# All five engines of a fused attention and token-mixer kernel pinned to one order of steps, and part of its TensorE work removed

## The chip, the cores and the metric

The kernel runs on one core of one Trainium2 chip. Time is device time in microseconds (us) of that core; every number called a time is the median of several executions, and every "span" is the length of the one profiled execution, from its first to its last instruction. Engines: PE is TensorE's matmul side, PEld its weight loads, DVE is VectorE, ACT is ScalarE, POOL is GpSimd, SP is SyncE, which here only issues transfers.

## The reference

For 8 batches (8 heads, 576 positions, head width 64) the reference adds two attentions, and sends the sum through a token mixer:

```python
q_d, k_d, v_d = (t.reshape(B, H, S//4, 4, D).mean(axis=3) for t in (q, k, v))
out_d     = softmax(q_d @ k_d.T / sqrt(D)) @ v_d            # coarse, 144 positions
out_up    = np.repeat(out_d, 4, axis=2)
out_local = softmax(where(|i-j| < 4, q @ k.T / sqrt(D), -1e9)) @ v   # band
x  = (out_up + out_local) as [B, 576, 512]
wq, wk = x @ w_q, x @ w_k                                   # 512 -> 64
out = relu((wq @ wk.T / sqrt(64)) @ x) @ w_out
```

The product `(wq @ wk.T) @ x` is computed as `wq @ (wk.T @ x)`, so the mixer has a 64 x 512 middle matrix, `M2`.

## The kernel before

All matmuls are in fp16. Each batch goes through a cast stage and three stages, whose steps are Python closures:

- **cast**: q, k, the remainder rows r, and v from fp32 to fp16, on GpSimd.
- **a**: transposes of q, k, r on TensorE (PSUM tiles `pq`, `pk`, `pr`), evacuations to `qT`, `kT`; fourfold sums on GpSimd (`qd`, `kd`); masked scores of the band (`psc`) and their exponential `E`; the coarse v (`pv`, giving `vd` and `vblk`).
- **b**: coarse scores (`pcs`), coarse output (`pca`, giving `od`), its transpose (`pod`), band output (`pav`, giving `x`), its transpose (`px`, giving `xT`).
- **c**: `pw` (x times w_q and w_k, giving `wT`), transposed parts (`pwk`, and `pwd` before, `pws` after, for the coarse part), `pm2` (`pm` in the traces), `pmx` and `pmr` (relu, giving `rmx`), and the output matmuls `po` and `pol`.

Two pools of PSUM tiles serve all of that: three tiles of two banks (`ps`) and two of one bank (`psm`). A step that needs a tile waits until the tile's earlier user has been evacuated.

Stages of three different batches are interleaved by a rule of proportions, and only TensorE keeps the order in which the program emits its instructions. What the other four engines do when is left to the compiler's scheduler:

```python
class _InOrder:                       # cut
    def __getattr__(self, name):
        f_ = getattr(self._engine, name)
        return lambda *a, **k: self._tc.keep_in_program_order(f_(*a, **k))

TEN_ = _InOrder(tc, nc.tensor)

def merge(stages):
    steps = []
    for i, s_ in enumerate(stages):
        tot, at = sum(c for c, _ in s_), 0.0
        for c, f_ in s_:
            steps.append(((at + c / 2) / tot, i, f_))
            at += c
    for _, _, f_ in sorted(steps, key=lambda e: e[:2]):
        f_()
# ...
for i in range(B + 2):
    if i + 1 < B: st[i + 1]["in"] = load(i + 1)
    m_ = []                           # stage_c(i-2), stage_b(i-1), stage_a(i), stage_cast(i+1)
    # ...
    merge(m_)
```

`pw` multiplies the coarse output at full length, each coarse column read four times:

```python
for i in range(2):
    for r in range(4):
        TEN_.matmul(p_[:, i, 0:288], wqk16[:, r, :],
                    _ap(odT, r * T + 72 * i, [[row(odT), 128], [1, 72], [0, 4]]), start=(r == 0), stop=False)
    for r in range(4):
        TEN_.matmul(p_[:, i, 0:288], wqk16[:, r, :], xT[:, r, 288*i:288*i + 288], start=False, stop=(r == 3))
```

Many matmuls use a part of the array, for example 64 rows, 16 rows or 16 columns, so that TensorE changes the tile shape (rows x columns of the array in use) often.

The softmax here doesn't subtract the row's maximum and nothing guards it: scores larger than these inputs give would overflow.

## Time and profile before

The time before is 227.07 us (226.61 to 227.63, three runs).

| | before |
|---|---|
| span | 225.2 us |
| TensorE busy | 180.7 us, 80% |
| period of one batch in mid-kernel (start of `po` to start of `po`) | 23.06 us |
| TensorE work per batch, waits left out (estimate) | about 21.3 us |
| TensorE waits per batch (estimate) | about 1.8 us |
| first `pw` of the kernel | 51.8 us |

These are lines of the profile's page of the kernel before: busy time of each engine with its share and number of instructions; the busy tenths of TensorE in 40 slices of the span; the clock granted to TensorE in the same slices; the mean busy share of the DMA engines; and the shares of the chain of work that ended last.

```profile
span 225.2 us, 6421 instructions
...
PE 180.7 (80%) x2752; PEld 112.2 (50%) x2752; DVE 104.3 (46%) x262; ACT 103.1 (46%) x137; POOL 115.9 (51%) x131
...
PE   0336077759988998899898989898989998999681
...
PEclk9999999857999999999999999999999999999999
...
PE 49%; DVE 17%; POOL 16%; ACT 10%; issue 3%; DMA 3%; POOLq 0%; DVEq 0%; ACTq 0%
```

The row of digits shows two kinds of time. From slice 10 on (about 51 us) TensorE is at 8 or 9 tenths nearly without interruption: there the period is TensorE's own work plus a few short waits. Before that it is idle more than half the time. The chain gives GpSimd 16%; all its pieces on GpSimd lie in the first 73 us. (The row PEclk shows 9 where the profile holds no record of the clock. In this run the first record is at 36.4 us.)

The next lines are the windows view of the kernel before over two periods: start and end, length, busy us of each engine (and instructions), granted clock, DMA share, GB/s.

```profile
88.30:111.30 23.00, 21.47 (x344) 13.31 (x344) 12.02 (x29) 12.64 (x18) 13.52 (x13) 1.00 0.81 214
111.30:134.40 23.10, 21.52 (x345) 13.36 (x345) 12.11 (x29) 12.71 (x18) 13.62 (x13) 1.00 0.80 208
```

TensorE is busy 21.5 us of 23, no other compute engine more than 13.6. And here is what TensorE waited for in the whole of that run (some groups left out; us in total, times, longest):

```profile
PE pv L27 <- POOL v_0_136 L163: 9.0, 3, 7.9
PE pq_230 L27 <- POOL q_142 L156: 8.6, 1, 8.6
PE pr L27 <- POOL r_144 L158: 4.1, 1, 4.1
PE pv L27 <- POOL v_1_138 L163: 3.7, 3, 2.6
PE psc L27 <- DVE rmx L445: 2.1, 6, 0.3
PE pw L27 <- DVE xT L368: 1.5, 7, 0.3
PE pv L27 <- POOL v_2_140 L163: 1.1, 2, 0.6
```

The long ones (7.9, 8.6, 4.1 and 2.6 us) are single waits of the start, for GpSimd's casts. The rest come once per batch: 0.6 us at `pv` for GpSimd's cast of v, up to 0.3 us at `psc` and at `pw`. So waits are small in mid-kernel, and to make it much shorter TensorE must have less to do.

### The profile page before, as it was taken

How to read it: one execution, taken by the hardware profiler on the slowest of the kernel's cores; microseconds unless marked ns; L12 is line 12 of the kernel's file. 1: busy time of each engine (PE TensorE's matmuls, PEld its weight loads, DVE VectorE, ACT ScalarE, POOL GpSimd, SP SyncE). 2: the span in 40 equal slices, each digit the busy share in tenths (PEclk: the TensorE clock that was granted, in tenths of full speed). 3: DMA queues.
4: the chain of work that ended last, by engine and by line, in shares of the span. 5: the costliest groups of instructions: out<-in, count | busy, mean ns of one | idle time of the engine just before them, and what ended most of it. 6: DMA issues, size and time to landing. Idle time of an engine off the chain costs nothing.

```text
span 225.2 us, 6421 instructions
## 1 busy us (share of the span) xinstructions
PE 180.7 (80%) x2752; PEld 112.2 (50%) x2752; DVE 104.3 (46%) x262; ACT 103.1 (46%) x137; POOL 115.9 (51%) x131
## 2 busy tenths in 40 slices
PE   0336077759988998899898989898989998999681
PEld 0223046536555664566455745574557455656330
DVE  6005046523466337354726472646364546477022
ACT  2154036413843593458444853475456554331331
POOL 3587991993079607970698059904990393000000
PEclk9999999857999999999999999999999999999999
DMA  6999989979974599659974997599731022104105
GB/s 184 288 198 328 317 165 263 266 150 243 249 173 146 156 349 163 194 146 341 170 207 129 332 175 167 189 309 206 195 136 27 3 92 82 41 3 157 53 0 210
DMA packets 74027, 40.54 MB, mean 180 GB/s; under 512 B 52432, under 2 KB 68880, under 8 KB 74000
## 3 DMA queue, kind: packets, MB, share of 16 engines
q1 hardware_dynamic: 73920, 40.12, 68.7%
q8 instruction: 21, 0.34, 0.7%
q14 instruction: 6, 0.05, 0.1%
q10 hardware_dynamic: 80, 0.03, 0.1%
HBM read 30.67 MB, written 9.44 MB: 178 GB/s over the span
## 4 chain that ended last, share of the span: by engine, by line
PE 49%; DVE 17%; POOL 16%; ACT 10%; issue 3%; DMA 3%; POOLq 0%; DVEq 0%; ACTq 0%
PE po L27 11%; PE pw L27 8%; ACT kT L184 5%; DVE xT L368 5%; DVE rmx L445 4%; PE pav L27 3%; PE pmx L27 3%; PE pod L27 3%; DMA q_72<-in_q_dram 3%; PE psc L27 3%; DVE os L470 3%; PE px L27 2%; PE pca L27 2%; POOL qd L207 2%; PE pwd L27 1%
## 5 line engine op out<-in xcount | busy, mean ns | idle before, releaser
L27 PE MATMUL po<-wo_98,rmx 128*128 128x512 f16 x128 | 30.4, 380 | 2.3 <-ACT rmx L443 0.6
L27 PEld LDWEIGHTS <-rmx 128*128 128x128 f16 (+1 forms) x160 | 14.1, 100 | 18.1 <-ACT rmx L443 0.7
L368 DVE COPY xT<-px 128x928 f16<-128x928 f16 (+1 forms) x32 | 14.3, 453 | 11.4 <-PE px L27 11.0
L348 DVE RECIPROCAL rz<-pav 128x8 f32<-128x8 f32 x40 | 8.1, 202 | 24.7 <-PE pav L27 23.9
L27 PEld LDWEIGHTS <-wqk_97 128*128 128x128 f16 x128 | 12.2, 100 | 6.5 <-DVE xT L368 2.9
L313 DVE RECIPROCAL rc<-pca 128x8 f32<-128x8 f32 (+1 forms) x16 | 3.2, 201 | 22.6 <-PE pca L27 22.6
L468 ACT COPY os<-po 128x1024 f32<-128x1024 f32 x8 | 8.1, 1012 | 11.8 <-PE po L27 10.6
L445 DVE TENSOR_SCALAR rmx<-pmx 128x1024 f16<-128x1024 f32 x8 | 9.8, 1224 | 7.3 <-PE pmx L27 7.3
L27 PE MATMUL pw<-odT,wqk_97 128*128 128x288 f16 x64 | 11.0, 297 | 1.5 <-DVE xT L368 1.5
L470 DVE COPY os<-po 128x1024 f32<-128x1024 f32 x8 | 9.7, 1216 | 4.8 <-ACT os L468 3.0
L443 ACT ACTIVATE rmx<-pmx 128x1024 f16<-128x1024 f32 x8 | 8.2, 1024 | 5.9 <-PE pmx L27 5.9
L27 PE MATMUL pw<-xT,wqk_97 128*128 128x288 f16 x64 | 10.8, 293 | 0.0
L27 PE MATMUL psc<-id_67,neg 64*128 64x232 f16 (+1 forms) x80 | 8.7, 280 | 2.1 <-DVE rmx L445 2.1
L329 DVE COPY odT<-pod 128x576 f16<-128x576 f16 x8 | 3.7, 458 | 14.4 <-PE pod L27 14.4
L27 PE MATMUL psc<-qT,kT 64*64 64x58 f16 (+1 forms) x640 | 10.3, 200 | 0.0
L482 ACT COPY ol<-pol 64x512 f32<-64x512 f32 x8 | 4.6, 579 | 11.6 <-PE pol L27 11.6
L27 PEld LDWEIGHTS <-kT 64*64 64x64 f16 x640 | 7.6, 114 | 4.4 <-issue 3.8
L27 PE MATMUL pq_230<-id_67,q_142 128*128 128x128 f16 x16 | 1.9, 312 | 8.6 <-POOL q_142 L156 8.6
L27 PE MATMUL pv<-v_0_136,P_149 128*32 128x512 f16 x3 | 1.3, 449 | 9.0 <-POOL v_0_136 L163 9.0
L27 PE MATMUL pol<-wo_98,rmx 128*64 128x512 f16 x32 | 8.4, 385 | 0.0
L242 ACT ACTIVATE E_0_122<-psc 128x928 f16<-128x928 f32 x4 | 3.8, 946 | 9.7 <-PE psc L27 9.7
L256 ACT CAST vd_0_195<-pv 128x512 f16<-128x512 f32 x4 | 2.4, 588 | 12.5 <-PE pv L27 12.5
(561 smaller groups left out, 518.3 us busy)
## 6 DMA issues: line engine op xcount, KB each, us to landing
out_dram<-os SPq DMA_DIRECT2D x16, 512.0 KB, 3.0
v_75<-in_v_dram SPq DMA_DIRECT2D x10, 128.0 KB, 4.2
v_215<-in_v_dram SPq DMA_DIRECT2D x10, 128.0 KB, 4.4
v_401<-in_v_dram SPq DMA_DIRECT2D x10, 128.0 KB, 3.7
v_779<-in_v_dram SPq DMA_DIRECT2D x10, 128.0 KB, 3.9
v_1258<-in_v_dram SPq DMA_DIRECT2D x10, 128.0 KB, 4.2
v_1737<-in_v_dram SPq DMA_DIRECT2D x10, 128.0 KB, 3.7
v_2216<-in_v_dram SPq DMA_DIRECT2D x10, 128.0 KB, 3.8
```

What stands on the lines that cost most here:

```text
L27: return lambda *a, **k: self._tc.keep_in_program_order(f_(*a, **k))
L184: nc.scalar.copy(t_[:, :, 0:512].rearrange("p j (t f) -> p j t f", f=4), g["p" + key].rearrange("p a (j f t) -> p (a j) t f", j=2, f=4))
L207: nc.gpsimd.tensor_tensor(qd, s_[:, :, :, 0], s_[:, :, :, 1], op=ALU.add)
L242: nc.scalar.activation(E.rearrange("p a n h w -> p a (n h) w")[:, :, :, 0:w], p_[:, :, 0:len(pr_) * W].rearrange("p a (x w) -> p a x w", w=w),
L329: nc.vector.tensor_copy(odT, p_[:, 0:4 * T].rearrange("p (r t) -> p r t", r=4))
L348: nc.vector.reciprocal(rz[:, n], _ap(p_, 64, [[row(p_), 128], [512, 2], [65, 4]]))
L368: nc.vector.tensor_copy(g["xT"][:, 2 * i:2 * i + 2, o:o + m * w].rearrange("p r (m w) -> p r m w", m=m), p_[:, :, lo:lo + 64 * m].rearrang ...
L443: nc.scalar.activation(d_, p_, ACTF.Relu)
L445: nc.vector.tensor_scalar_max(d_, p_, 0.0)
L468: nc.scalar.copy(os_, p_)
L470: nc.vector.tensor_copy(os_, p_)
L482: nc.scalar.copy(ol_, p_[0:64])
```

## The change

The intent is to fix the order of steps on all five engines. The order is one list of steps with batch lags, said to come from a search over a model of the program; evacuations of PSUM are divided between ScalarE and VectorE by a table. The diff is larger than that description: it also removes and pads work. This is its core, with cuts:

```diff
-    TEN_ = _InOrder(tc, nc.tensor)
+    pe = _InOrder(tc, nc.tensor)
+    sp = _InOrder(tc, nc.sync)
+    pool = _InOrder(tc, nc.gpsimd)
+    act = _InOrder(tc, nc.scalar)
+    dve = _InOrder(tc, nc.vector)
 # ... every instruction of a step goes through these; load() is split in load_qk and load_v
+    load_qk(1)                       # q and k of batch 1 are asked for before w_out
 # ... batch 0: casts of q, r on dve, of k on act; its k sums on dve; w_out's casts on act
+    EVAC = {"qT": "a", "kT": "a", "rem": "d", "vd0": "a", "odT": "a", "xT0": "d", "xT1": "d",
+            "wTd": "a", "wk": "d", "wd": "a", "M2": "a", "mx0": "a", "mx1": "d", "mxr": "a",
+            "og0": "a", "og1": "a", "ol": "d"}
 # ... before: odT, mxr, og1 on VectorE; wk, ol on ScalarE
-                    TEN_.matmul(p_[:, i, 0:288], wqk16[:, r, :],            # fourfold coarse half of pw
-                                     _ap(odT, r * T + 72 * i, [[row(odT), 128], [1, 72], [0, 4]]), ...)
+        def wtd():                                                          # once, on 144 columns
+            for r in range(4):
+                pe.matmul(p_[:, 0:T], wqk16[:, r, :], odT[:, r, :], start=(r == 0), stop=(r == 3))
+            evac("wTd", wd, p_[:, 0:T])
+            dve.tensor_tensor(wT[...], p_[:, :, 0:288] ..., wd broadcast 4x, op=ALU.add)
-                for od, lo, hi in ((g["od0"], 0, 128), (g["od1"], 128, T)):  # second one 16 rows
-                    TEN_.transpose(p_[:, r * T + lo:r * T + hi], od[:, 128*r:128*r + 128], id16[...])
+                for i in range(2):                                           # both 128 rows
+                    pe.transpose(p_[:, 256*r + 128*i:256*r + 128*i + 128], g["od"][i][...], id16)
 # ... the same kind of padding in pcs, pca, pws, pm2, pmx, pmr, pol
-    merge(m_)
+    ORDER = [
+        (-2, "og1"), (-1, "wtd"), (0, "sums"), (1, "cast_qk"), (-1, "wt"), (0, "vd"), (0, "mask0"),
+        (0, "score0"), (-1, "wks"), (2, "load_qk"), (1, "cast_v"), (0, "mask1"), (-1, "wkt"), (0, "score1"),
+        (0, "mask2"), (0, "av0"), (-1, "m2"), (0, "av3"), (0, "score2"), (0, "av1"), (-1, "mx0"), (0, "av2"),
+        (0, "cs0"), (-1, "mx1"), (0, "cs1"), (0, "av4"), (0, "weights"), (-1, "mxr"), (1, "tq"), (0, "ca0"),
+        (2, "load_v"), (-1, "og0"), (0, "ca1"), (1, "tk"), (1, "tr"), (-1, "ol"), (0, "xt0"), (0, "xt1"),
+        (0, "odt"),
+    ]
+    for i in range(-3, B + 3):
+        for lag, name in ORDER:
+            if 0 <= i + lag < B and (i + lag, name) not in done:
+                steps[i + lag][name]()
```

So three things come together: (1) less TensorE work, by the single coarse half and by fewer changes of tile shape; (2) another order; (3) pins on four more engines.

## The prediction

> **What bounds it now.** In mid-kernel a batch takes 23.06 us (the starts of the output matmuls `po`: 88.3, 111.3, 134.4, 157.4 us in the timeline). TensorE is the busiest engine there (18.5 to 19.0 of every 20 us, by windows; VectorE 10.4 to 10.9, ScalarE 9.8 to 11.6, GpSimd 10.5 to 13.6). From start-to-start times of matmuls at 60 to 160 us: 216 ns for 512 columns, 123 for 288, 56 for 128. Each change of tile shape adds about 95 ns (512 columns: 311 instead of 216; 128 columns: 150 instead of 56), about 44 changes per batch. [...] Summed, TensorE needs about 21.3 us per batch, and about 1.8 us are waits (px to pv 0.64, pav to psc 0.42, psc to po 0.32, pcs to pw 0.26). Outside the steady part: `pq` of the third batch starts only at 55.0 us (two batches started; GpSimd casts and sums, in the chain of waits, and DMA share 0.9 to 1.3), and after the last batch's `pw` at 207 us come 18 us.
>
> **What the change does.**
> 1. `pw` loses its fourfold coarse half: 8 matmuls of 288 go, 4 of 144 come: 0.98 - 0.25 = -0.73 us.
> 2. Padding of pod, pca, pcs, pm, pmx, pol to full shape, and the order, leave about 17 shape changes: roughly -2.5 us. My sum for the new order is 18.3 us of TensorE per batch.
> 3. VectorE takes the coarse add, wk and ol; ScalarE odT, wTd, mxr, og1: ScalarE 13.6, VectorE 12.3, GpSimd 13.8 us per batch. None binds. DMA packets took 18.2 us of 16 engines per batch, so DMA stays under, nearly filled.
> 4. All engines are strictly ordered. Walking the order by hand with these durations (0.26 us from last matmul to evacuation, 3 double-bank PSUM buffers), `av1` waits 0.9 us for the exp of `score2` (same buffer), cs0, mx1, av4 together 0.8, `tq` 0.5 for the relu of mx1: 2.2 us of waits. Period 20.5 us.
> 5. The last stage lags one iteration less. Start: `vd` stands first, so TensorE waits for v's cast, about 20 us for batch 0 and about 40 for batch 1 (its v lands about 38, as before). ScalarE waits for wo (now behind q, k of batch 1), around 29 us. TensorE is idle before 40 us and may run at the low clock there (before: 0.50 at 45 to 50 us).
>
> **Sum.** Second iteration ends at about 59 us; five iterations of 20.5 to 161.5; one without the next batch's transposes, 18.5, to 180; last stage, output and landing 18 to 19: 199; times run 2 us over the span: **200 us**, 8 in 10 between **190** and **211**. Chances: faster by over 2% 0.95, within 2% 0.04, slower 0.01.
>
> **What would show it.** Mid-kernel period 20 to 21 us; `pw` 8 per batch; TensorE gaps at pav and pq, ended by ScalarE's E and VectorE's rmx; TensorE above 60% of the chain; a TensorE gap before batch 1's `pv` ended by GpSimd's v cast; matmul busy sum lower than 180.7 us.
>
> **What would make it wrong.** DMA not keeping up once a batch takes 20 us (then the period is above 21 and gaps end on casts that waited for DMA); waits overlapping less than in my walk; or the start being better hidden (then down to 190).

## The result and the profile after

The changed kernel takes 193.46 us (193.05 to 194.9, four runs) against 227.05 us. The ratio is 0.852, with a 95% interval of 0.847 to 0.857. The outputs are correct.

The lines of the page after, in the order used above; the line "q8 instruction" is of the DMA queues (packets, MB, share of the 16 engines) and is needed later:

```profile
span 192.7 us, 6374 instructions
...
PE 155.5 (81%) x2720; PEld 104.0 (54%) x2720; DVE 114.8 (60%) x286; ACT 110.7 (57%) x140; POOL 107.7 (56%) x122
...
PE   0034448885899989998999899989998999898790
...
PEclk9999555999789999999999999999999999999997
...
q8 instruction: 21, 0.34, 0.7%
...
PE 68%; DVE 17%; ACT 7%; issue 4%; POOL 2%; ACTq 0%; DVEq 0%
```

TensorE's busy time fell by 25.2 us, its share of the chain rose from 49 to 68%, and GpSimd nearly left the chain (16 to 2%). Two periods in the windows view after:

```profile
93.30:112.60 19.30, 18.52 (x345) 12.44 (x342) 12.32 (x29) 13.22 (x18) 11.96 (x13) 1.00 0.95 239
112.60:131.90 19.30, 18.52 (x345) 12.43 (x342) 12.32 (x29) 13.23 (x18) 13.47 (x12) 1.00 0.92 241
```

A period is 19.30 us (before 23.06), and the DMA engines are now 92 to 95% busy in it (before 80%). They are not the limit yet: none of TensorE's waits between 88 and 157 us ends on a transfer or on a cast. TensorE's waits of the whole run (some groups left out):

```profile
PE pq_236 L27 <- DVE q_229 L27: 12.6, 1, 12.6
PE pv L27 <- POOL v_0_147 L27: 5.2, 1, 5.2
PE psc L27 <- DVE vblk_201 L27: 2.8, 1, 2.8
PE pav L27 <- issue: 2.3, 1, 2.3
PE pmx L27 <- ACT E_0_135 L27: 1.2, 3, 0.4
PE pmx L27 <- ACT E_1_145 L27: 1.2, 3, 0.4
```

Only one wait of size is left per batch, 0.4 us at the first `pmx`, which takes over the PSUM tile of the last band score and has to wait for its exponential E. Two more are 0.2 us each (`pcs` for an x, `pav` for Ec). With what the start-to-start times of the matmuls leave for waits, a period reads as follows; the work column is an estimate, summed from start-to-start times of the trace with the waits taken out.

| | period | TensorE work | waits | shape changes per batch in the trace |
|---|---|---|---|---|
| before | 23.06 | 21.3 | 1.8 | 40 |
| after | 19.30 | 18.2 | 1.05 | 18 |

One of the 18, from 112 to 128 rows in `pm`, costs only 10 ns (226 instead of 216 ns between starts), so 17 count.

Where the 32.5 us of span went, by the starts of `pw`: 12.0 us until the first `pw` (51.8 to 39.8), 19.1 us between the first and the last (155.4 to 136.3), 1.4 us after the last (18.0 to 16.6).

What a change of tile shape costs can be read from the timeline after. Columns are start in us, length of one in us, engine, source line, operation, output and inputs, tile shape, form, number; the bracket gives idle time before it and what ended it.

```profile
45.03 0.38 PE L27 MATMUL pm_847<-x_444,wk_206 128*128 128x512 f16 x1
45.25 0.38 PE L27 MATMUL pm_847<-x_543,wk_206 128*128 128x512 f16 x1
45.56 0.38 PE L27 MATMUL pav<-v_1_149,E_1_141 64*64 64x65 f16 x12
...
45.97 0.23 PE L27 MATMUL pav<-v_1_149,E_1_143 64*64 64x65 f16 x3
48.52 0.38 PE L27 MATMUL pav<-v_1_149,E_1_143 64*64 64x65 f16 x13 [2.33 <-issue]
```

The 512-column matmuls start 0.21 to 0.22 us apart, but the first 64 x 64 one starts 0.31 us after the last of them: about 95 ns more for the change from 128\*128 to 64\*64. The last two lines show another thing: a hole of 2.3 us between matmuls of one and the same tile, with nothing that the profile could name as waited for. It is taken up in the experiments on the start.

### The profile page after: what moved, and what is told of

Same layout as the page of the kernel before. It is cut to its first block, busy times and chain, and to the rows that moved or that the text cites. A ratio compares the mean times of both kernels' runs of the same rounds, so it can differ in the third digit from the quotient of the medians.

```text
span 192.7 us, 6374 instructions
## 1 busy us (share of the span) xinstructions
PE 155.5 (81%) x2720; PEld 104.0 (54%) x2720; DVE 114.8 (60%) x286; ACT 110.7 (57%) x140; POOL 107.7 (56%) x122
## 4 chain that ended last, share of the span: by engine, by line
PE 68%; DVE 17%; ACT 7%; issue 4%; POOL 2%; ACTq 0%; DVEq 0%
PE po L27 15%; PE psc L27 6%; PE pav L27 5%; PE pw L27 4%; PE px L27 4%; PE pca L27 4%; PE pol L27 4%; DVE kd_127 L27 3%; PE pv L27 2%; PE pcs L27 2%; ACT kT L27 2%; PE pod L27 2%; DVE rz L27 1%; PE pws L27 1%; PE pwd L27 1%
## 5 line engine op out<-in xcount | busy, mean ns | idle before, releaser
L27 ACT COPY os<-po 128x1024 f32<-128x1024 f32 x16 | 16.2, 1012 | 14.7 <-issue 8.3
L27 PE MATMUL po<-wo_91,rmx_227 128*128 128x512 f16 x64 | 15.3, 379 | 0.6 <-ACT rmx_227 L27 0.6
L27 PE MATMUL po<-wo_91,rmx_212 128*128 128x512 f16 x64 | 15.1, 379 | 0.0
L27 DVE COPY xT<-px 128x928 f16<-128x928 f16 (+1 forms) x32 | 13.8, 451 | 0.6
L27 PE MATMUL pq_236<-id_67,q_229 128*128 128x128 f16 x16 | 1.9, 312 | 12.6 <-DVE q_229 L27 12.6
L27 PEld LDWEIGHTS <-rmx_227 128*128 128x128 f16 x80 | 7.2, 98 | 8.1 <-ACT rmx_227 L27 0.7
L27 PE MATMUL psc<-qT,kT 64*64 64x58 f16 (+1 forms) x640 | 11.4, 198 | 0.0
L27 PEld LDWEIGHTS <-rmx_212 128*128 128x128 f16 x80 | 7.2, 98 | 6.6
L27 PEld LDWEIGHTS <-wqk_90 128*128 128x128 f16 x96 | 8.3, 98 | 3.7 <-issue 0.9
L27 ACT COPY odT<-pod 128x448 f16<-128x448 f16 (+1 forms) x16 | 5.6, 402 | 6.3 <-PE pod L27 6.3
L27 PE MATMUL pw<-xT,wqk_90 128*128 128x288 f16 x64 | 9.2, 286 | 0.0
L27 PEld LDWEIGHTS <-q_229 128*128 128x128 f16 x16 | 1.6, 146 | 12.6 <-DVE q_229 L27 12.6
L27 POOL CAST v_0_147<-v_79 128x2560 f16<-128x2560 f32 x1 | 3.1, 3129 | 9.3 <-DMA w_92<-in_moe_w_k_dram 9.3
L27 DVE TENSOR_TENSOR wT_219<-pw,wTd 128x576 f16<-128x576 f32 x4 | 3.0, 758 | 8.6 <-ACT wTd L27 8.6
L27 DVE COPY ol<-pol 64x512 f32<-64x512 f32 x8 | 5.5, 682 | 4.3 <-PE pol L27 4.3
L27 DVE TENSOR_TENSOR wT_204<-pw,wTd 128x576 f16<-128x576 f32 x4 | 3.0, 758 | 8.0 <-ACT wTd L27 6.6
L27 DVE TENSOR_SCALAR rmx_227<-pmx 128x1024 f16<-128x1024 f32 x4 | 4.9, 1224 | 4.1 <-PE pmx L27 4.1
L27 POOL CAST v_1_149<-v_255 128x2560 f16<-128x2560 f32 x1 | 2.3, 2323 | 8.6 <-DMA v_255<-in_v_dram 8.6
```

## The experiments

Three theories of the gain were open. The first: less TensorE work explains it (25 us less busy time). The second: the order explains it. The third: the pins explain it, above all one on some engine whose order the scheduler gets wrong. Experiments e1, e4, e9 and e10 take order and pins apart; e2 and e3 put work back in the new order; e5 undoes the division of evacuations; e6, e7, e8, e11 and e12 are on what is left. Each is an edit of the changed kernel, and all gave correct outputs. The kernel before took 227.69 us in the rounds of e1 to e4, 226.94 in those of e5 to e8, 227.48 in those of e9 to e12.

### e1: only TensorE pinned, all else as after

```diff
-    sp = _InOrder(tc, nc.sync)
-    pool = _InOrder(tc, nc.gpsimd)
-    act = _InOrder(tc, nc.scalar)
-    dve = _InOrder(tc, nc.vector)
+    sp, pool, act, dve = nc.sync, nc.gpsimd, nc.scalar, nc.vector
```

> The changed kernel, but only TensorE is pinned; the scheduler orders the other four engines again. In the built program it changes little: ScalarE puts wTd before the copy of og1, GpSimd casts v before q and k, VectorE's setup is shuffled. Theory A (the gain is less TensorE work plus a TensorE order that leaves few waits): 193.5 us, within 192 to 197. Theory B (pinning all five engines to one order is what pays): above 200 us, with new TensorE gaps in mid-kernel and a period above 20 us instead of 19.3.

Measured: 249.72 us, ratio 1.095 (1.090 to 1.100). The new order without the pins is slower than the kernel before, and 56 us slower than with them. This is in theory B's range. One group of TensorE's waits in this run stands out, and so does the row of the granted clock:

```profile
PE pv L27 <- POOL v L257: 41.4, 8, 7.2
...
PEclk9995569559995799659985899569975999579999
```

`pv` waits for the cast of v in every batch, up to 7.2 us. GpSimd's timeline of one period of e1 shows why:

```profile
120.57 2.11 POOL L295 TENSOR_TENSOR sum<-qT 128x1152 f32<-128x1152 f16 x1 [13.81 <-DVE qT L238]
...
127.70 2.32 POOL L257 CAST v<-v 128x2560 f16<-128x2560 f32 x1
...
147.98 2.11 POOL L295 TENSOR_TENSOR sum<-qT 128x1152 f32<-128x1152 f16 x1 [13.73 <-DVE qT L238]
```

and GpSimd's timeline of the changed kernel, one period:

```profile
112.49 2.32 POOL L27 CAST v_2_151<-v_1970 128x2560 f16<-128x2560 f32 x1 [3.79 <-DMA out_dram<-os]
116.57 2.11 POOL L27 TENSOR_TENSOR sum_2573<-qT 128x1152 f32<-128x1152 f16 x1 [1.76 <-DVE qT L27]
...
123.71 1.89 POOL L27 CAST q_2583<-q_2183 128x2048 f16<-128x2048 f32 x1
```

In the changed kernel the cast of v stands before the sums, early enough for `vd`, which the new order puts first. Left to the scheduler, GpSimd does the sums of q and k first, which need that batch's transposes, and only then the cast of v, which `pv` needs. TensorE, pinned, stops at `pv`; so the next batch's transposes come late; so GpSimd sits idle 13.8 us. A ring through two engines makes the period 27.4 us, though no engine is full. The low clock is part of it: from 73 us on it is 0.5 for 10.2 of each 27.3 us, and from the start of `pv` to that of `pr` (the last transposes before the sums) TensorE takes 17.0 us here and 13.6 in the changed kernel. So an estimated 3.4 us of the 8.1 us by which the period is longer come from the clock; in e9, where the wait is gone, the clock stays at 1.0 in mid-kernel.

### e9: TensorE and GpSimd pinned

```diff
-    sp = _InOrder(tc, nc.sync)
     pool = _InOrder(tc, nc.gpsimd)
-    act = _InOrder(tc, nc.scalar)
-    dve = _InOrder(tc, nc.vector)
+    sp, act, dve = nc.sync, nc.scalar, nc.vector
```

> TensorE and GpSimd pinned, ScalarE, VectorE and the DMA queue left to the scheduler. In the slow run with TensorE alone pinned, the scheduler had put GpSimd's cast of v behind the sums of the same batch, while TensorE's order has vd, which needs that cast, first in the iteration: tr(b), sums 7.1 us, cast 2.3 us, vd(b) became a loop of 27.4 us. Theory C (that one place on GpSimd is the whole loss): back to 193 to 197 us, period 19.3 to 19.5. Theory B (each pinned engine matters): above 200 us.

Measured: 196.3 us (195.95 to 197.06), ratio 0.864 (0.860 to 0.867), period 19.6 us. The time is in theory C's range, the period just above its 19.5. Pinning GpSimd gives back 53 of the 56 us that e1 lost. Pins on SyncE, ScalarE and VectorE together are worth the last 3 us: the period of e9 is 0.33 us longer than after from the second on, all of it between `pv` and the next `psc`, where its trace has a wait that it puts down to VectorE's wT (0.3 us per batch) and the trace after has none.

### e2: the coarse half back in `pw`

```diff
-        def wtd(): ...                # 4 matmuls of 144 columns, added on VectorE
+        for i in range(2):            # in pw: 8 matmuls of 288 columns on the fourfold odT
+            for r in range(4):
+                pe.matmul(p_[:, i, 0:288], wqk16[:, r, :], _ap(odT, ..., [[row(odT), 128], [1, 72], [0, 4]]), ...)
-            dve.tensor_tensor(wT..., p_..., wd..., op=ALU.add)
+            dve.tensor_copy(wT..., p_...)
```

> The coarse half goes back into the 288-column matmuls of pw (16 instead of 8 per batch), wtd goes, VectorE copies instead of adding; the order stays. Theory A (TensorE is still the bound in every batch, so its work counts in full): 8 x 123 - 4 x 62.5 = +0.73 us per batch, period 20.0 us, total 199 us (197.5 to 200.5). Theory B (the order makes the gain; this work is hidden by waits that exist anyway, about 1 us per batch): below 196 us.

Measured: 200.87 us (200.11 to 202.16), ratio 0.882 (0.878 to 0.887), period 20.3 us. That is just above theory A's range; theory B is out. The single coarse half is worth 7.4 us in the new order, 1.0 us per batch, more than the 0.73 us that the matmuls alone make. In the traces these are 0.98 - 0.25 = 0.73 us, as expected; the other 0.26 us lie between `pv` and the next `psc`, a wait for wT as in e9.

### e3: ten shape changes per batch put back

```diff
-                    pe.transpose(p_[...128 columns...], g["od"][1][:, 128*r:128*r + 128], id16)
+                pe.transpose(p_[...32 columns...], g["od"][1][96:128, 128*r:128*r + 128], id16[96:128, 96:128])
-                pe.matmul(p_, rmx[:, r * S + 512:r * S + 640], wo16[:, r, :], ...)       # pol, 128 wide
+                pe.matmul(p_[0:64], rmx[:, r * S + 512:r * S + 576], wo16[:, r, :], ...)  # 64 wide
```

> The changed kernel with two paddings undone: od1's transposes take 32 rows (8 more changes of tile shape per batch) and pol takes 64 columns (2 more). No matmul is added; four get fewer columns. Theory A (a change of tile shape costs about 95 ns of TensorE): +10 x 0.095 - 0.1 = about +0.8 us per batch, period 20.1 us, total 200 us (197 to 202). Theory B (shape changes are free, only columns and order count): 193 us or slightly less.

Measured: 200.47 us (199.52 to 200.97), ratio 0.879 (0.875 to 0.884), period 20.2 us, in theory A's range. Ten more shape changes per batch cost 7.0 us: 7.0 / 80 is 88 ns for each, beside the 95 ns of the trace. The padding that e3 undoes costs at most an estimated 0.22 us per batch (four transposes of 128 columns, which start 56 ns apart in the trace; 512 columns start 216 ns apart on 64 columns of the array as on 128), so it is nearly free here beside the 0.88 us per batch that leaving these matmuls small costs. In the new order, work taken from TensorE comes back as time almost one for one.

### e4: the new work in the old order, only TensorE pinned

The steps of the changed kernel are emitted by the old rule of proportions; `wtd` and `wt` share the old weight of `pw`, a mask and its score that of the old score.

```diff
-    sp = _InOrder(...); pool = ...; act = ...; dve = ...
+    sp, pool, act, dve = nc.sync, nc.gpsimd, nc.scalar, nc.vector
-    ORDER = [ ...the searched list... ]
+    ORDER = old_order()      # stage c at lag -2, b at -1, a at 0, casts at +1, merged by shares
```

> The changed kernel's steps, work, padding and evacuation split in the old order (the proportional merge of the stages, last stage two iterations behind), with only TensorE pinned, as before. 21 shape changes per batch in the built program instead of 17 (before: 39 in the trace). Theory A (most of the gain is TensorE work taken away): TensorE needs about 18.6 us per batch plus waits as before, 1.8 us: period 20.4 us, total 203 to 212. Theory B (the searched order is most of the gain): period above 21.5 us, total above 217.

Measured: 213.15 us (212.06 to 214.15), ratio 0.935 (0.929 to 0.941), period 22.1 us: the total lies between what the two theories expected, the period in theory B's range. Its TensorE waits between 88 and 157 us, where the trace after has 0.4 us per batch at `pmx` and little else:

```profile
PE pv L27 <- ACT E L337: 2.0, 3, 0.7
PE po L27 <- DVE x L450: 1.7, 3, 0.6
PE pmx L27 <- ACT M L230: 1.6, 3, 0.5
PE pwk L27 <- DVE wT L499: 1.4, 3, 0.5
PE pav L27 <- DVE rmx L234: 1.3, 3, 0.4
```

So a period of e4 is an estimated 18.6 us of work (three or four more shape changes than after) and 3.4 us of waits. The old order had 2.7 us of work per batch removed and paid only 1.0 us; 1.6 us turned into waits for evacuations (3.4 us per batch against 1.8). That TensorE, with less work in between, comes to each evacuation sooner is the reading of these waits, not measured. The list ORDER places some other batch's matmuls between a matmul and the one that needs its evacuation; that this is what removes the waits is read from the list and the two tables of waits, no run isolates it.

By the starts of `pw`, the 14.5 us by which the span of e4 (210.7 us) is shorter than before are 3.9 at the start (first `pw` at 47.9 us), 9.2 between the first `pw` and the last, and 1.4 at the end. Of the other 18 us to the changed kernel 8.1 are at the start and 9.9 between the first `pw` and the last. What moving batch 0's casts off GpSimd and asking for q and k of batch 1 early bring at the start was not measured apart: e4 has both.

### e10: the same, all five engines pinned

```diff
-    ORDER = [ ...the searched list... ]
+    ORDER = old_order()      # all five _InOrder kept; the weights' casts at the end of the list
```

> The old order of steps with the new work, now with all five engines pinned to it (w_out's cast at the end of the first iteration). With only TensorE pinned this took 213 us at a period of 22.1, about 3.4 us of it waits of TensorE for evacuations of the step just before. Theory A (the waits lie in the order of the steps themselves): 208 to 216 us. Theory B (pinning the other engines repairs them): below 205 us.

Measured: 224.0 us (222.95 to 225.15), ratio 0.985 (0.981 to 0.989), and nearly the same waits in mid-kernel as e4, with a period of 21.7 to 22.8 us. Neither expectation held. The loss against e4 is in the start: `pwd` of the first batch starts at 57.5 us, in e4 at 45.9. TensorE's waits in the first 60 us of e10 include these two:

```profile
PE pcs L27 <- POOL qd L27: 10.4, 1, 10.4
PE pcs L27 <- POOL kd L27: 6.5, 1, 6.5
```

Pinned GpSimd holds the sums of a batch behind casts of the next batch, whose data have not landed: its timeline has the sums of batch 0 starting at 30.0 us, behind casts that waited for q and k from memory until 22.7 and 27.6 us, and those of batch 1 at 49.7 us, behind a cast that waited for k until 47.3 us. Pins are not good in themselves: they keep a good order and a bad one alike. (The place of the weights' casts differs between e4 and e10 too; the two waits above do not end on them, but its share was not measured apart.)

The four runs together: old order, TensorE pinned 213.2; old order, all pinned 224.0; new order, TensorE pinned 249.7; new order, all pinned 193.5. The gain belongs to the pair, and neither half alone gives it.

### e5: the old division of evacuations

```diff
-  "odT": "a", "wk": "d", "mxr": "a", "og1": "a", "ol": "d"
+  "odT": "d", "wk": "a", "mxr": "d", "og1": "d", "ol": "a"
```

> The changed kernel and order, all pinned, with the old division of evacuations (odT, mxr, og1 back on VectorE; wk and ol back on ScalarE). By the durations read, ScalarE goes from 13.6 to about 12.9 us per batch and VectorE from 12.3 to about 13.2, both far under the 19.3 us period. Theory A (TensorE-bound with about 1 us of waits, evacuations mostly off the path): 193 to 198 us. Theory B (the division is part of what makes the order work): above 200 us, with new TensorE waits on VectorE's og1 or odT.

Measured: 195.09 us (194.68 to 195.85), ratio 0.859 (0.856 to 0.863), period 19.5 us. That is inside theory A's range. The division of evacuations, which the change names, is worth about 1.6 us; the intervals of the two ratios overlap slightly, and the period (19.48 us against 19.30 in the traces) is the firmer sign. Part of it may be the start, where this run waited 5.8 us for `vblk` and the profiled run after 2.8.

### e8: the last band score earlier

The one wait of size left, `pmx` for E, should go if the last score stands three steps earlier.

```diff
-        (0, "mask2"), (0, "av0"), (-1, "m2"), (0, "av3"), (0, "score2"), (0, "av1"), (-1, "mx0"), ...
+        (0, "mask2"), (0, "score2"), (0, "av0"), (-1, "m2"), (0, "av3"), (0, "av1"), (-1, "mx0"), ...
```

> Only the order: score2 goes before av0 instead of after av3. Its exp then runs under m2, and mx0 no longer waits for it (0.41 us per batch, in the waits of TensorE); instead mx0 may wait up to 0.3 us for M2, since less work lies between m2 and mx0. Theory A (what waits are left are PSUM buffers held by exps): period 19.0 to 19.2 instead of 19.3 us, 191 to 193 us. Theory B (the searched order is already the best in this neighbourhood): 193.5 us or more.

Measured: 196.17 us (195.85 to 196.71), ratio 0.864 (0.861 to 0.867), period 19.45 us. Theory A failed. The wait is gone, but the one at `pcs` has grown from 0.2 us per batch (for an x) to 0.6 (for rmx); the 0.2 us at `pav` were there before. TensorE's waits of e8 between 88 and 157 us are all in two lines:

```profile
PE pcs L27 <- ACT rmx L27: 2.2, 4, 0.6
PE pav L27 <- ACT Ec L27: 0.8, 4, 0.2
```

Moving one step of the list did not remove the wait but moved it, and the period grew by 0.16 us. The three two-bank PSUM tiles serve the steps in turn, so each step that moves can also change whose evacuation the next ones wait for.

### The start: e6, e7, e11, e12

After the change TensorE first works at 12.6 us and runs at 3 to 8 tenths until 43 us. The next lines are from VectorE's timeline after: it adds the k sums of batch 0, beside a busy GpSimd.

```profile
18.22 1.36 DVE L27 TENSOR_TENSOR sum_296<-kT 128x1152 f32<-128x1152 f16 x1 [1.06 <-ACT kT L27]
19.61 5.71 DVE L27 TENSOR_TENSOR kd_127<-sum_296 128x116 f16<-128x116 f32 x4
25.24 1.96 DVE L27 TENSOR_TENSOR kdt_129<-sum_296 128x112 f16<-128x112 f32 x1
27.12 0.75 DVE L27 TENSOR_TENSOR vblk_201<-pv,blk 128x256 f16<-128x256 f32 x2
```

The same adds on GpSimd, in e6:

```profile
26.59 1.39 POOL L27 TENSOR_TENSOR kd<-sum 128x116 f16<-128x116 f32 x4
27.94 0.37 POOL L27 TENSOR_TENSOR kdt<-sum 128x112 f16<-128x112 f32 x1
```

And the same adds on VectorE in e10, where GpSimd casts v until 21.75 us and then does nothing until 22.66 us:

```profile
19.61 2.85 DVE L27 TENSOR_TENSOR kd<-sum 128x116 f16<-128x116 f32 x4
22.38 0.26 DVE L27 TENSOR_TENSOR kdt<-sum 128x112 f16<-128x112 f32 x1
```

Four small adds take 5.71 us on VectorE beside a busy GpSimd and 1.39 us on GpSimd. While VectorE adds, GpSimd casts v in 3.13 us (2.32 in other places). The trace of e10 isolates the slow ones: of its four adds the one that begins during GpSimd's cast takes 2.28 us, and the three that run while GpSimd is silent take 0.27 us each. In the trace after, the two slowest adds (2.28 and 2.18 us), the fourth (1.22 us) and the one of `kdt` (1.96 us) each end 0.13 to 0.14 us after the GpSimd instruction during which they began; the third began at 23.91 us, between two GpSimd instructions (23.85 to 23.93 us), and takes 0.27 us. So in these two traces the time of such an add goes by when that GpSimd instruction ends, hardly by its own size. Why it does is not shown. `vblk` comes behind the adds on the same engine, and TensorE waits 2.8 us for it (5.8 to 6.5 us in the profiled runs of e5 and e9).

**e6** puts the adds on GpSimd.

```diff
-                add = (dve if i == 1 and b == 0 else pool).tensor_tensor
+                add = pool.tensor_tensor
```

> Batch 0's sums of k go back from VectorE to GpSimd. On VectorE the four kd adds took 1.43 us each (5.71 us) beside GpSimd's reads; on GpSimd the same adds take 0.35 us each. TensorE's 2.8 us gap at 25.1 to 27.9 us (mask2 waiting for VectorE's vblk) should go, but batch 1's v lands at 38.1 us in any case and holds TensorE at vd(1) near 40.9 us. Theory A (start held by v(1)'s landing): 192.5 to 194 us. Theory B (that gap is on the path): 191 us or less.

Measured: 194.72 us (192.82 to 195.44), ratio 0.859 (0.854 to 0.863). The wait for `vblk` is gone, yet the median did not fall: it is just above theory A's range, and its ratio's interval overlaps that of the changed kernel. The next batch's `pv` starts at 41.1 us (after: 40.9), since v of batch 1 lands at 38 us and has to be cast: what was gained is waited for again there.

**e7** adds to e6 that v of batch 1 is asked for before w_out, whose casts move to a later place.

```diff
+    load_v(1)                                     # before w_out
-        ... (0, "av1"), (-1, "mx0") ...
+        ... (0, "av1"), (-1, "weights"), (-1, "mx0") ...   # w_out's casts; w_q, w_k's cast stays
```

> As the previous one, and v of batch 1 is loaded before the 1 MB of w_out; w_out's casts move to just before mx0 of batch 0. v(1) should land about 4 us earlier (34 instead of 38.1) and batch 1's first pv start near 36.5 instead of 40.9 us; the steady part stays. Theory A (the start is held by DMA order): 188 to 190.5 us. Theory B (start held by something else, GpSimd's casts or the low clock): 192 us or more.

Measured: 193.62 us (193.26 to 193.96), ratio 0.853 (0.850 to 0.856). `pv` of batch 1 did start 2.1 us earlier (38.8 us), and `pw` of batch 1 at 60.7 instead of 62.4. The expected 188 to 190.5 us were missed all the same. A line of e7's waits in the first 60 us:

```profile
PE pav L27 <- issue: 2.7, 1, 2.7
```

This is the hole of the timeline above, at 43.92 to 46.83 us here and 46.00 to 48.52 us in the run after. It lies between matmuls of one tile, with no semaphore to wait for. In the traces at hand (before 1.3 us; after 2.5; e1 1.1; e2 2.1; e6 three of 0.7 to 0.9; e7 2.9; e10 1.8; e11 0.8; e12 1.0, between starts of matmuls) each such hole ends 1.3 to 1.7 us after a packet of 16 KB of DMA queue 8 ends, the queue that the page calls "instruction". That queue moves 21 packets, 0.34 MB, before and after, while TensorE starts 5504 and 5440 matmuls and weight loads: 262 and 259 for each packet. A count over all 14 traces gives nearly the same: from the end of one packet to the end of the next TensorE starts 252 on the mean (246 before, 253 after). And the holes of these two lie one such count apart: before, TensorE had started 703 of them when it stopped at 42.04 us, and the second packet had ended 1.6 us before the hole did; after, it had started 957 at 46.00 us, and the third packet ended 1.5 us before the hole did. So it is an estimate from these counts, not more, that the queue carries TensorE's own instructions, about 250 to a packet, and that at such a hole TensorE had run out of them. What made these packets late is not shown, and no run changed the queue alone.

**e11** tests another reading of the start: the granted clock was 0.5 from 19.9 to 33.6 us (and, after the hole, from 50.6 to 54.0 us). Useless matmuls (44 before the first transposes, 24 after them) keep TensorE busy.

```diff
+    def warm(n):
+        p_ = ps(name="pdum")
+        for j in range(n):
+            pe.matmul(p_[:, j % 2, :], id16, <id16 repeated to 512 columns>, start=True, stop=True)
+    # warm(44) before batch 0's "tq", warm(24) after its "tr"
```

> The changed kernel plus matmuls without use on the identity: 44 of 512 columns before batch 0's first transposes and 24 after its last, so that TensorE does not idle there. Its granted clock was 0.5 from 19.9 to 33.6 us. Theory A (the start is held by v(1)'s landing at 38.1 and cast at 40.4): within 1 us of the changed kernel, 192.5 to 194.5, though the clock is 1.0 after 20 us. Theory D (the low clock holds the start): 190.5 us or less.

Measured: 194.2 us (192.78 to 195.36), ratio 0.853 (0.849 to 0.858): no gain. But the edit lifted the low clock only in part: it was granted in full from 4.8 to 25.3 us, and at 0.5 again from 25.3 to 35.5 us. And `pv` of batch 1 started 1.6 us after its cast had ended (41.99 and 40.36 us), so there TensorE's own chain was late. What a start at full clock throughout would save stays open. (The clock row of e5 has no slow slice, but its first record is at 37.9 us: its 128-column transposes start 107 ns apart until then.)

**e12** joins e7 and the warm-up of e11.

> The same useless matmuls on the kernel that loads v(1) before w_out and sums on GpSimd (193.6 us without them; its TensorE clock was 0.5 from 20.5 to 34.2 us and batch 1's pv started at 38.8 us). Theory A with both limits lifted: pv(1) at about 36.8 us, total 190 to 192 us. Theory E (the next limit is the instruction stream: a 2.9 us gap inside av1 of batch 1 that ends 1.5 us after a 16 KB packet of the instruction queue): pv(1) earlier but the total unchanged, 193 us or more.

Measured over five rounds: 191.8 us (190.93 to 193.2, six runs), ratio 0.844 (0.840 to 0.848). The time is in theory A's range; `pv` of batch 1 came at 39.9 us, not at the expected 36.8. That is the lowest median, 1.7 us under the changed kernel, but the two were measured in different rounds and their intervals (0.840 to 0.848, 0.847 to 0.857) just touch. Its only such hole is one of 1.0 us, at 123 us, and `po` of the first batch starts at 51.3 us instead of 54.6. It is a small and probable gain; which half of the edit brings it, e7 having none by itself, is not settled.

## Why the prediction was right

The predicted time was 200 us, 190 to 211; measured were 193.46. Point by point:

- **What bounds it: right.** TensorE's own work, at 21.3 us of a 23.06 us period. The count of shape changes was too high: "about 44" against 40 in the trace.
- **Work removed: right in sum.** The predicted 18.3 us of TensorE work per batch is 18.2 by the trace after. The coarse half's matmuls are the predicted 0.73 us in the traces of e2 and after (e2 adds a wait of 0.26). Shape changes that cost fell by 23, to the predicted 17, which at the 88 to 95 ns of e3 and the traces is 2.0 to 2.2 us, not "roughly -2.5": the start of that count was too high.
- **None of the other engines binds: right.** Predicted 13.6, 12.3 and 13.8 us per batch for ScalarE, VectorE and GpSimd; the windows show 13.2, 12.3 and 12.0 to 13.5.
- **"2.2 us of waits. Period 20.5 us": this is the term that was mis-sized.** Measured are about 1.05 us and 19.30 us, below the predicted 20 to 21. The walk had `av1` waiting 0.9 us for the exponential of `score2`; in the trace `av1` starts at once (so it seems to get the PSUM tile that `av0` has already left), and `mx0` waits for the exponential instead, 0.4 us. The wait of `tq` for `mx1` does not appear. Five iterations at 20.5 would be 102.5 us; they took 96.5 (60.4 to 156.9 us). The following one was predicted at 18.5 and took 17.3.
- **Start and end: right within 1.5 us, the start in part by luck.** The end of the second iteration was predicted at 59 and came at 60.4. But these 60.4 us hold a hole of 2.3 us and a stretch of low clock after it (an estimated 0.9 us, by the same matmuls one period later) that the prediction did not have; without them the start would have been 1.8 us shorter than predicted. The last stage with output and landing took 18.5, predicted 18 to 19. `pv` waited for the cast of v, as said, until 21.8 us. For batch 1 the cast ended at 40.4 and `pv` started at 40.9, as said, but without a visible gap before it. ScalarE's wait for w_out at 29 us is not there: its casts ran at 33.2 and 34.1 us, behind other work. The low clock came (0.5 from 19.9 to 33.6 us); what it cost is open (e11).
- **The sum:** 60.4 + 96.5 + 17.3 + 18.5 is the 192.7 us of span. Against the predicted terms the start is +1.4, the five periods are -6.0, the next iteration is -1.2.
- **What would show it:** `pw` has 8 matmuls per batch, TensorE has 68% of the chain, its busy sum is 155.5 us: all as said. The gaps at `pav` and `pq` were not; the gap is at `pmx`.
- **What the prediction did not see:** it treated less work, order and pins as a list of separate gains. The runs show otherwise. In the old order the changed kernel's work gains 14.5 us of the 34, some 4 us of it at the start (e4), and 1.6 of the 2.7 us removed per batch turn into waits. The order without pins loses 22 us against before (e1), because GpSimd's cast of v then comes too late; and pins on the old order lose the start (e10). It did not see the slow adds on VectorE, nor the holes in TensorE's instructions.

## What to carry to other kernels

When one engine is nearly full, removing work from it pays only if the order gives it something else to do while the others evacuate: check the waits per period after the removal, not only the busy sum, and be ready for the removed time to come back as many waits of half a microsecond. An order for one engine is only as good as the order of the engines that feed it; pin first the engine whose late step closes a ring (here GpSimd with its cast of v; pinning it was worth 53 us, the low clock that came with the waits included), and look at the start of the kernel when pinning, because a strict order also queues ready work behind data that have not landed. Pad small matmuls to the shape of their neighbours where TensorE binds, since ten shape changes per batch cost about as much here (7.0 us) as the largest block of arithmetic that was removed (7.4 us).

## Sizes that the traces show

- A change of tile shape costs about 95 ns in the trace after (a 64 x 64 matmul starts 0.31 us after a 512-column one, where the next 512-column one starts after 0.21 to 0.22 us), and 88 ns by e3; from 112 to 128 rows it is 10 ns.
- In mid-kernel, at full granted clock, matmuls of one shape start 216 ns apart at 512 columns, 123 ns at 288 and 56 ns at 128.
- A transpose of 128 columns takes 0.22 us in mid-kernel, and sixteen in a row start 56 ns apart. Their rate follows the granted clock: in the trace after, those of batch 1 start 107 ns apart until 33.51 us and 56 ns apart from 33.59 us, and the record of the clock goes from 0.5 to 1.0 at 33.55 us. In e9 TensorE runs nothing but the program's transposes from 11.48 us on; they start 107 ns apart until 14.5 us, where the first record of the clock shows it granted in full, and 55 to 56 ns apart after it. So it was granted in full 3.0 us after the first of them (3.3 us in e6, from 12.63 to 15.9 us; 3.9 us in the trace after, from 12.63 to 16.48 us).
- With GpSimd silent the adds of 116 columns start 0.19 us apart on VectorE (e10) and 0.34 us on GpSimd (1.8 times), and the large add takes 1.36 against 2.11 us (1.55 times). Beside a busy GpSimd the four small adds were four times slower on VectorE than on GpSimd (5.71 against 1.39 us).
- TensorE stood still for 0.7 to 2.9 us between starts of matmuls, with nothing named as waited for, in 9 of 14 traces, each time until 1.3 to 1.7 us after a 16 KB packet of the queue "instruction".
